# Products that nobody reads, put into TensorE's queue at three places of a fused attention and feed-forward kernel

## The chip, the cores and the metric

The kernel runs on one core of a Trainium2 chip. Its time is the device time of that core in microseconds (us). Three runs gave 560.56, 560.72 and 562.95 us, with a median of 560.72 us. The engines are called by the short names of the profile: PE is TensorE (PEld its weight loads), DVE is VectorE, ACT is ScalarE, POOL is GpSimd and SP is SyncE, which issues the DMAs.

## The reference

The reference computes attention with a memory term, and then a feed-forward layer on every token. B, H, S and D are 4, 8, 576 and 64; the layer has 2304 tokens, 512 columns and an inner width of 2048.

```python
scores = where(causal, -1e9, q @ k.T / sqrt(D));  a = softmax(scores)
local  = a @ v
q_p    = phi(q)                                   # phi(x) = where(x > 0, x, exp(x) - 1) + 1
mem    = (q_p @ M_prev) / (q_p @ z_prev + 1e-6)
x      = g * mem + (1 - g) * local                # g = sigmoid(beta), per head
out    = relu(x @ w_in) ** 2 @ w_out              # x as 2304 x 512
```

## The kernel before

**Work.** Attention runs in units: one unit is one batch, one pair of heads and some of the four 128-row query tiles. The feed-forward layer runs in blocks of 256 tokens. Block 0 holds the first 64 tokens of all four batches; its attention is computed ahead of everything by `first_tokens` in two groups of two batches (group 0 and group 1), so that block 0 can start while the units go on.

**Weights.** The weights come in 32 pieces of 128 x 512 floats of 64 bits, 512 KB each. `to_float` makes a 32-bit float tile `fc` of each piece: POOL or ACT (L200, L202) takes the low word, ACT (L205) the high word, and DVE (L207) joins them. Four pieces make a bundle: bundles 0, 2, 4, 6 are pieces of `w_in`, bundles 1, 3, 5, 7 of `w_out`. For each bundle `weight_scale` lets PE sum squares of the four pieces in a PSUM tile `gr` (L233), DVE takes a maximum of them (L236), PE spreads it over the partitions (L214) and DVE takes a maximum again (L215). From that come the scales `win_s` or `wout_s`, and `halves` makes the fp16 high part of each piece on ACT (L251) and its rest on DVE (L252): tiles w0 to w31. The name `kap` stands for the maxima of a `w_out` bundle, `win_e` for those of a `w_in` bundle.

**Group outputs.** `outputs(g)` transposes the exponentials (PE, `px`), copies them (ACT, `wx`, L391), multiplies with v (PE, `pv`, L395), and then DVE (L396, L397) and ACT make the fp16 rows `hl` that a DMA transposes into `xT`, the input of block 0.

**A unit.** PE writes scores (`sp`, L588), DVE masks them and takes maxima (L609), ACT takes exponentials (L631), PE transposes them (`pxa`, L648), ACT copies (`aF`, L653), PE multiplies with v (`acc`, L697), DVE adds to `feat` (L700). Unit 0 is the first of these; it has two query tiles.

**Order.** A list scheduler places every instruction on its engine's queue when the program is built, by estimated times; on the chip each engine works through its queue in order. Helpers such as `later` add an order without a wait: the instruction is placed behind the last one that `gate` names. PSUM tiles with one tag share buffers: `gr` and `up` (the first products of a block, L1000 to L1002) have two 2 KB buffers together, `px`, `pv`, `nm` and `oacc` two others. `fc` has 12 buffers, the raw pieces 7.

Of the kernel before, what the change touches and what calls it, by code (L numbers as in the profile page):

```python
# [8 lines left out]
F32 = mybir.dt.float32  # L9
F32R = mybir.dt.float32r  # L10
F16 = mybir.dt.float16
BF16 = mybir.dt.bfloat16
# [10 lines left out]
P = 128  # L23
# [58 lines left out]
WE = 8  # L82
WE2 = 16
WH = 11
AFTER = mybir.DependencyInfo(mybir.DependencyClass.NoSync, mybir.DependencyReason.DATA)
WHOLE = mybir.DependencyInfo(mybir.DependencyClass.Sync, mybir.DependencyReason.DATA)

# [13 lines left out]
def fused_kernel(ctx: ExitStack, tc: tile.TileContext, t0_d, kk_d, qv_d, beta, w_in, w_out, out):  # L101
    nc = tc.nc
    w_in = w_in.bitcast(U32)
    w_out = w_out.bitcast(U32)
    cp = ctx.enter_context(tc.tile_pool(name="cp", bufs=1))
# [6 lines left out]
    make_identity(nc, ident)  # L112
    identb = cp.tile([P, P], BF16, name="identb")
    nc.vector.tensor_copy(identb, ident)


    win_e = cp.tile([P, 4], F32, name="win_e")
# [50 lines left out]
    gate = {}  # L168

    def later(eng, x):  # L170
        if eng in gate:
            tc.add_manual_dep(x.ins, gate[eng].ins.name, AFTER, reason="first tokens lead")
        return x
# [19 lines left out]
    def to_float(n):  # L193
# [15 lines left out]
        )  # L209
        raw.pop(n)  # L210

    def over_partitions(x, al):

        nc.tensor.matmul(al, x.bitcast(BF16)[:, 1:2].to_broadcast([P, P]), identb, start=True, stop=True)  # L214
        nc.vector.reduce_max(out=x, in_=al, axis=AX.X)  # L215
# [9 lines left out]

    def weight_scale(g, w_is_out):

        gr = ps.tile([P, 2, P], F32, tag="up", name="gr", bufs=2)
        for k, n in enumerate(range(4 * g, 4 * g + 4)):
            x = fc[n].bitcast(BF16).rearrange("p (n t) -> p n t", t=2)[:, :, 1]  # L230
            for c in range(4):
                xc = x[:, c * P : (c + 1) * P]
                nc.tensor.matmul(gr[:, 0], xc, xc, start=k == c == 0, stop=k == c == 3)  # L233
        j = slice(g // 2, g // 2 + 1)
        x = kap[:, j] if w_is_out else win_e[:, j]
        nc.vector.reduce_max(out=x, in_=gr[:, 0], axis=AX.X)  # L236
        over_partitions(x, gr[:, 1])
        if w_is_out:
            root(x, 0x7E000000, 2, 2.0 ** (96 - 6))
            nc.vector.tensor_tensor(out=wout_s[:, j], in0=x, in1=x, op=ALU.mult)  # L240
            nc.vector.reciprocal(wout_s[:, j], wout_s[:, j])
            nc.vector.tensor_tensor(out=x, in0=x, in1=win_e[:, j], op=ALU.mult)
        else:
            root(x, 0x7F000000, 1, 2.0 ** (64 - 12))
            nc.vector.reciprocal(win_s[:, j], x)
# [67 lines left out]
    def first_tokens(tp, ahead):  # L313
# [23 lines left out]
        def pairs():  # L337
            return [(i, slice(h * D, (h + 1) * D)) for i in range(GN) for h in range(2)]
# [47 lines left out]
        def outputs(g):  # L386
            ex = tp.tile([P, GN, D], F32, tag="wx", name="wx", bufs=2)
            px = ps.tile([P, GN, D], F32, tag="acc", name="px0", bufs=2)
            for i, hd in pairs():
                nc.tensor.matmul(px[hd, i], et[g][hd, i], ident[hd, hd], start=True, stop=True)  # L390
            gate["s"] = nc.scalar.copy(ex, px)  # L391
            v, x, y = part(g, TV), ft[g], et[g]
            pv = ps.tile([P, GN, D], F32, tag="acc", name="pv0", bufs=2)
            for i, hd in pairs():
                gate["t"] = nc.tensor.matmul(pv[hd, i], ex[hd, i], v[hd, i], start=True, stop=True)  # L395
            nc.vector.tensor_tensor(out=y, in0=pv, in1=st[g][:, :, None].to_broadcast(bc), op=ALU.mult)  # L396
            nc.vector.tensor_tensor(out=x, in0=x, in1=y, op=ALU.add)  # L397
            xb = x.rearrange("p (b i) d -> p b (i d)", b=GB)
            hl = mo.tile([P, 2, GB, NP * D], F16, tag="hl", name="hl", bufs=2)
            ss, q, s = (tp.tile([P, GB], F32, tag=t, name=t, bufs=2) for t in ("s0", "qn", "sn"))  # L400
            for b in range(GB):
                nc.scalar.activation(hl[:, 0, b], xb[:, b], AF.Square, accum_out=ss[:, b : b + 1])
            nm = ps.tile([P, GB], F32, tag="acc", name="nm0", bufs=2)
            nc.tensor.matmul(
                nm, both.rearrange("p h x -> p (h x)"), ss.bitcast(BF16).rearrange("p (n t) -> p n t", t=2)[:, :, 1], start=True, stop=True
            )
            root(q, 0x7F000000, 1, 2.0**64 * XSC, nm)
            nc.vector.reciprocal(s, q)
            for b in range(GB):
                hi, lo, s1 = hl[:, 0, b], hl[:, 1, b], s[:, b : b + 1]  # L410
                gate["s2"] = nc.scalar.activation(hi, xb[:, b], AF.Copy, scale=s1)
                gate["v2"] = nc.vector.scalar_tensor_tensor(
                    out=lo, in0=xb[:, b], scalar=s1, in1=hi, op0=ALU.mult, op1=ALU.subtract
                )
            nc.sync.dma_start_transpose(out=xT[:, g], in_=hl.rearrange("p x b n -> p (x b n)"))
            for b in range(GB):
                hd = slice(b * D, (b + 1) * D)
                nc.scalar.activation(tok0[hd, g : g + 1], q[hd, b : b + 1], AF.Square, scale=WSC / HSC)
# [39 lines left out]
    def attention(b, p, tiles, ld, after, early, sfull, full, ap, ap_early):  # L458
# [163 lines left out]
        for i in [t for t in TORD if t in tiles]:  # L622
# [15 lines left out]
            if full:  # L638
# [3 lines left out]
                for b0 in range(0, 2 * nb, 4):  # L642
                    bn = min(4, 2 * nb - b0)
                    px = ps.tile([P, 4, P], F32, tag=PXT, name="pxa", bufs=2)
                    for x in range(bn):
                        h, c = divmod(b0 + x, nb)
                        c0, cw = cols[c]
                        nc.tensor.transpose(px[:cw, x, :n], e[:n, h, c0 : c0 + cw], ident)  # L648
                    lo = [x for x in range(bn) if (b0 + x) % nb == 0]
                    for x0, xn, pn in [(x, 1, D) for x in lo] + runs([x for x in range(bn) if x not in lo]):  # L650
                        dst, src = aT[:pn, b0 + x0 : b0 + x0 + xn, :n], px[:pn, x0 : x0 + xn, :n]
                        if PXE[b0 // 4] == "a":
                            nc.scalar.copy(dst, src)  # L653
                        else:
                            nc.vector.tensor_copy(dst, src)
# [293 lines left out]
    def moe(n):  # L949
# [43 lines left out]
        for j in range(NF // 2):  # L993
            need(1 + 8 * (j // 2 + 1))
            up = ps.tile([P, 2, BLK], F32, tag="up", name="up", bufs=2)
            for u in range(2):
                f = 2 * j + u
                uo = up[:, u].rearrange("p (g b q) -> p g b q", g=2, b=GB) if lead else up[:, u]
                for k in range(NK):
                    nc.tensor.matmul(uo, w_in_op(f, k, 0), x_op(k, 0), start=k == 0, stop=False)  # L1000
                    nc.tensor.matmul(uo, w_in_op(f, k, 0), x_op(k, 1), start=False, stop=False)  # L1001
                    nc.tensor.matmul(uo, w_in_op(f, k, 1), x_op(k, 0), start=False, stop=k == NK - 1)  # L1002
# [166 lines left out]
```

## Time and profile before

| | |
|---|---|
| median of 3 runs | 560.72 us |
| profiled execution | 560.21 us |
| its span, first to last instruction | 558.4 us |
| mean granted clock of TensorE | 0.976 of full |
| busy: PE, DVE, ACT, POOL | 523.7, 453.5, 410.0, 47.7 us |

The profiled execution takes 1.8 us more than its span, before the first and after the last instruction. Busy shares are averages over stages with different limits. PE is busy for 94% of the span, and without a gap from 70 to 100 us; before 70 us the weights are being made, and DVE and ACT are the engines that hardly pause. The granted clock has two levels, 1.00 (2.4 GHz) and 0.50 (1.2 GHz).

### The profile page before, as it was taken

The page shows a single profiled execution, that of the slowest core. Times are in us where ns is not written, and L with a number is a line of the kernel's source. Part 1 is how long each engine was busy: PE and PEld are TensorE (multiplying, and loading weights), DVE is VectorE, ACT ScalarE, POOL GpSimd, SP SyncE. Part 2 cuts the span into 40 slices and gives each one's busy share as a digit, 9 for nine tenths or more (in the row PEclk, how much of TensorE's full clock was granted, in tenths as well). Part 3 has the DMA queues.
Part 4 walks back from the last instruction along what each step waited for, and adds up shares of the span by engine and source line. Part 5 has one row for each costly group of instructions (what it writes and reads, how often), then busy time and mean ns, then how long its engine had stood idle before and what let it go on. Part 6 is the DMA issues. An engine that isn't in the chain of part 4 may idle for free.

```text
span 558.4 us, 12645 instructions
## 1 busy us (share of the span) xinstructions
PE 523.7 (94%) x4767; PEld 370.1 (66%) x4767; DVE 453.5 (81%) x1414; ACT 410.0 (73%) x883; POOL 47.7 (9%) x36
## 2 busy tenths in 40 slices
PE   4678999998999999999989999999999999999996
PEld 4555767756676776667756777667766766447776
DVE  6898978998999989999977878888686788745645
ACT  3699996875879889989877777888666734566252
POOL 2556420011010000000000000000000000000000
PEclk9965999999999999999999999999999999999999
DMA  8975922477778958979657376481745320100002
GB/s 305 406 274 191 329 80 69 103 143 172 129 144 174 208 136 144 193 151 204 119 103 154 113 138 123 76 141 50 114 92 81 89 44 2 39 1 1 1 1 75
DMA packets 133133, 71.38 MB, mean 128 GB/s; under 512 B 115408, under 2 KB 121552, under 8 KB 133072
## 3 DMA queue, kind: packets, MB, share of 16 engines
q1 hardware_dynamic: 133072, 70.57, 53.9%
q8 instruction: 37, 0.61, 0.4%
q14 instruction: 24, 0.20, 0.1%
HBM read 37.53 MB, written 4.72 MB: 76 GB/s over the span
## 4 chain that ended last, share of the span: by engine, by line
PE 37%; DVE 29%; ACT 20%; DMA 8%; issue 3%; POOL 1%; SPq 0%; ACTq 0%; DVEq 0%
DVE e L609 6%; ACT e L631 6%; PE seven L861 5%; DVE a L673 5%; PE oacc L972 4%; DMA aT<-a 4%; PE oacc L971 4%; PE oacc L973 4%; ACT a L671 3%; PE up L1000 3%; PE up L1002 3%; PE up L1001 3%; PE seven L833 2%; PE seven L834 2%; PE seven L832 2%
## 5 line engine op out<-in xcount | busy, mean ns | idle before, releaser
L1000 PE MATMUL up<-xT,w 128*128 128x256 f16 x448 | 123.4, 275 | 3.0 <-DMA xT<-hl 2.2
L1002 PE MATMUL up<-xT,w 128*128 128x256 f16 x448 | 123.4, 275 | 0.0
L1001 PE MATMUL up<-xT,w 128*128 128x256 f16 x448 | 123.3, 275 | 0.0
L631 ACT ACTIVATE e<-e,mx 128x320 f32<-128x320 f32 (+3 forms) x128 | 77.4, 605 | 49.3 <-DVE mx L609 22.9
L971 PE MATMUL oacc<-w,gh 128*128 128x512 f16 x224 | 85.0, 379 | 1.9 <-ACT gh L1009 1.9
L972 PE MATMUL oacc<-w,gh 128*128 128x512 f16 x224 | 84.9, 379 | 0.0
L973 PE MATMUL oacc<-w,gl 128*128 128x512 f16 x224 | 81.2, 379 | 0.5 <-DVE gl L1012 0.5
L673 DVE SCALAR_TENSOR_TENSOR a<-e,a 128x128 f16<-128x128 f32 x116 | 64.7, 568 | 11.6 <-ACT a L671 10.3
L671 ACT ACTIVATE a<-e 128x128 f16<-128x128 f32 x116 | 54.9, 522 | 1.6 <-DMA aT<-a 1.0
L1000 PEld LDWEIGHTS <-w 128*128 128x128 f16 x448 | 44.3, 99 | 14.3 <-DMA xT<-hl 2.6
L1001 PEld LDWEIGHTS <-w 128*128 128x128 f16 x448 | 44.3, 99 | 12.0 <-issue 1.7
L1002 PEld LDWEIGHTS <-w 128*128 128x128 f16 x448 | 44.2, 99 | 8.4 <-issue 0.4
L697 PE MATMUL acc<-vs,aT 128*128 128x64 f16 x1138 | 42.5, 193 | 6.6 <-DMA aT<-a 5.2
L609 DVE CUSTOM_DVE_ANT_0 e<-sp,mask 128x320 f32<-128x320 f32 (+3 forms) x128 | 47.2, 419 | 0.8 <-PE sp L588 0.4
L1006 ACT ACTIVATE r<-up,gam 128x512 f32<-128x512 f32 x48 | 32.4, 674 | 20.9 <-PE up L1002 18.3
L697 PEld LDWEIGHTS <-aT 128*128 128x128 f16 x1138 | 38.9, 98 | 12.5 <-DMA aT<-a 7.8
L1012 DVE TENSOR_TENSOR gl<-r,gh 128x512 f16<-128x512 f32 x56 | 39.0, 697 | 5.3 <-ACT gh L1009 4.7
L971 PEld LDWEIGHTS <-gh 128*128 128x128 f16 x224 | 21.9, 98 | 23.5 <-ACT gh L1009 2.7
L973 PEld LDWEIGHTS <-gl 128*128 128x128 f16 x224 | 21.7, 98 | 22.4 <-DVE gl L1012 1.5
L861 PEld LDWEIGHTS <-g 128*128 128x128 f16 x336 | 32.9, 98 | 4.2
L200 POOL TENSOR_SCALAR raw<-raw 128x512 uint32<-128x512 uint16 x16 | 33.0, 2063 | 27.9 <-DMA raw<-in_w_in_dram 11.8
L1007 ACT ACTIVATE r<-r 128x512 f32<-128x512 f32 x56 | 34.9, 623 | 0.7
(192 smaller groups left out, 1061.5 us busy)
## 6 DMA issues: line engine op xcount, KB each, us to landing
raw<-in_w_in_dram SPq DMA_DIRECT2D x16, 512.0 KB, 6.9
raw<-in_w_out_dram SPq DMA_DIRECT2D x16, 512.0 KB, 7.1
vv<-in_qv_dram SPq DMA_DIRECT2D x16, 320.0 KB, 3.1
kd<-in_kk_dram SPq DMA_DIRECT2D x16, 288.0 KB, 3.1
out_dram<-o SPq DMA_DIRECT2D x12, 256.0 KB, 2.0
qm<-in_qv_dram SPq DMA_DIRECT2D x8, 321.0 KB, 3.0
qm<-in_qv_dram SPq DMA_DIRECT2D x8, 193.0 KB, 4.1
vv<-in_qv_dram SPq DMA_DIRECT2D x8, 192.0 KB, 3.1
```

Of the source, the lines that this page charges most:

```text
L609: x = nc.vector.tensor_tensor_reduce(out=e[:, h, ka:kb], in0=sps[:, h, cs], in1=mask[:, 448 - q0 + ka : 448 - q0 + kb], scale=-0.125, scal ...
L631: ex = nc.scalar.activation(e[:n, h, :ke], e[:n, h, :ke], AF.Exp, bias=bs, scale=-1.0, accum_out=sm[:n, h : h + 1])
L671: nc.scalar.mul(av[:, :, o0 : o0 + w], x, SC)
L673: nc.vector.scalar_tensor_tensor(out=av[:, :, o0 + w : o0 + 2 * w], in0=x, scalar=SC, in1=av[:, :, o0 : o0 + w], op0=ALU.mult, op1=ALU.sub ...
L697: nc.tensor.matmul(acc[:n, h], lhs[:, :n], rhs, start=x == 0, stop=x == len(mms) - 1)
L861: mms.append(nc.tensor.matmul(x[blk] if len(blks) == 1 else x[:, blk], g[j][:, i0, a, blk, p], t_side(j, p, m, i1), start=j == js[0] and p ...
L971: nc.tensor.matmul(acc[t], gh[:, u, ts], w_out_op(f, 0), start=f == f0, stop=False)
L972: nc.tensor.matmul(acc[t], gh[:, u, ts], w_out_op(f, 1), start=False, stop=False)
L973: nc.tensor.matmul(acc[t], gl[:, u, ts], w_out_op(f, 0), start=False, stop=f == f1)
L1000: nc.tensor.matmul(uo, w_in_op(f, k, 0), x_op(k, 0), start=k == 0, stop=False)
L1001: nc.tensor.matmul(uo, w_in_op(f, k, 0), x_op(k, 1), start=False, stop=False)
L1002: nc.tensor.matmul(uo, w_in_op(f, k, 1), x_op(k, 0), start=False, stop=k == NK - 1)
```

## The change

At three places PE now multiplies a tile of zeros (`wide`, set once by POOL) with the identity and writes to PSUM columns that nobody reads, or that the next product overwrites:

- in `weight_scale`, 4 products of 256 columns behind each of pieces 4, 5 and 6, into the unused second half of `gr` (which grows from 1 KB to 2 KB of the same 2 KB buffer);
- in `outputs(1)`, 12 products of 512 columns into `pv` ahead of the real ones;
- in block 0, 8 products of 512 columns into the first `up` tile ahead of the real ones.

Where the name "x" is in `gate` when such a product is recorded, it is placed behind the last transpose recorded of unit 0. That holds for the first and the third place. Pieces 5, 6 and 7 of bundle 1 are summed behind such products in one PSUM tile, so their sums move too.

```diff
+SPARE = {4: 4, 5: 4, 6: 4}
...
+    wide = cp.tile([P, 4 * P], BF16, name="wide")
+    nc.gpsimd.memset(wide, 0.0)
...
+    def spare(out, n, new=True):
+
+        c = out.shape[-1] // P
+        for _ in range(n):
+            mm = nc.tensor.matmul(out, identb, wide[:, : c * P], start=new, stop=new)
+            if "x" in gate:
+                later("x", mm)
+
...
-        gr = ps.tile([P, 2, P], F32, tag="up", name="gr", bufs=2)
+        gr = ps.tile([P, 4, P], F32, tag="up", name="gr", bufs=2)
...
                 nc.tensor.matmul(gr[:, 0], xc, xc, start=k == c == 0, stop=k == c == 3)
+            spare(gr[:, 2:].rearrange("p a b -> p (a b)"), SPARE.get(n, 0), False)
...
             pv = ps.tile([P, GN, D], F32, tag="acc", name="pv0", bufs=2)
+            spare(pv.rearrange("p i d -> p (i d)"), (0, 12)[g])
...
-                        nc.tensor.transpose(px[:cw, x, :n], e[:n, h, c0 : c0 + cw], ident)
+                        x_ = nc.tensor.transpose(px[:cw, x, :n], e[:n, h, c0 : c0 + cw], ident)
+                        if me == 0:
+                            gate["x"] = x_
...
             up = ps.tile([P, 2, BLK], F32, tag="up", name="up", bufs=2)
+            if lead and j == 0:
+                spare(up.rearrange("p u b -> p (u b)"), 8)
```

The instructions move with it. In the rows below the line numbers of the changed kernel are larger (L233 becomes L244, L214 L225, L236 L248, L215 L226, L207 L210, L252 L264, L700 L715, L697 L712, L648 L661, L588 L601, L1000 L1017), and the numbers behind the names are those of single tiles.

PE around group 1 of the first tokens, before: `gr_529` is bundle 1 (pieces 4 to 7 are `fc_479` to `fc_527`; one product of the four of each piece is shown), `px0_306` and `pv0_324` belong to `outputs(1)`.

```order
L233 MATMUL gr_529<-fc_479 128x128
...
L233 MATMUL gr_529<-fc_494 128x128
...
L233 MATMUL gr_529<-fc_514 128x128
...
L233 MATMUL gr_529<-fc_527 128x128
...
L390 MATMUL px0_306<-ident_67,w_272 64x64 x16
...
L214 MATMUL gr_529<-identb_72,kap_77 128x128
L395 MATMUL pv0_324<-tr1_110,wx_305 64x64 x16
```

The same place now: `gr_543` is bundle 1, with piece 4 alone; the row of `pv0_326` from `wide_74` stands 12 times.

```order
L244 MATMUL gr_543<-fc_493 128x128
...
L417 MATMUL nm0_262<-s0_257,both_83 128x2
L402 MATMUL px0_308<-ident_67,w_274 64x64 x16
...
L219 MATMUL pv0_326<-wide_74,identb_72 128x512
...
L408 MATMUL pv0_326<-tr1_112,wx_307 64x64 x16
```

The sums of pieces 5 to 7 and the spreading of `kap` have left this place, and the 12 products stand between `px` and `pv`.

PE from the transposes of unit 0 to block 0, before: `pxa_499` holds the transposes of its second tile, `acc_481` the sums of its first, `gr_649` is bundle 3.

```order
L697 MATMUL acc_481<-vv_135,aF_419 128x64 x4
...
L214 MATMUL gr_649<-identb_72,kap_77 128x128
L697 MATMUL acc_481<-vv_135,aF_419 128x64 x2
...
L648 MATMUL pxa_499<-ident_67,e_412 64x128
L648 MATMUL pxa_499<-ident_67,e_412 128x128
...
L1000 MATMUL up_690<-xT_108,w0_463 128x256
```

The same place now; `fc_508` is piece 5 and stands for three times four rows (pieces 5, 6, 7), each behind four products into `gr_543` from `wide_74`; `gr_675` is bundle 3; the row of `up_716` from `wide_74` stands 8 times.

```order
L661 MATMUL pxa_513<-ident_67,e_426 128x128
...
L219 MATMUL gr_543<-wide_74,identb_72 128x256
...
L244 MATMUL gr_543<-fc_508 128x128
...
L225 MATMUL gr_675<-identb_72,kap_79 128x128
...
L225 MATMUL gr_543<-identb_72,kap_79 128x128
...
L219 MATMUL up_716<-wide_74,identb_72 128x512
...
L1017 MATMUL up_716<-xT_110,w0_477 128x256
```

Bundle 1 now ends between the transposes of unit 0 and block 0, behind 12 products from `wide`, and 8 more stand ahead of the first product of block 0. The maxima of bundles 1 and 3 are both spread there.

DVE behind unit 0, now: `feat_396<-acc_530` adds the second tile of unit 0, `w12_700` is of bundle 3 and `w4_580` of bundle 1. Before, the rests w4 to w7 stood some 60 rows further up, among the scores of unit 0 (L609).

```order
L264 SCALAR_TENSOR_TENSOR w11_648<-fc_614,win_s_77,w11_648 128x512
L248 TENSOR_REDUCE kap_79<-gr_543 128x1
L226 TENSOR_REDUCE kap_79<-gr_675 128x1
...
L715 SCALAR_TENSOR_TENSOR feat_396<-acc_530,sm_428,feat_396 128x64 x2
L264 SCALAR_TENSOR_TENSOR w12_700<-fc_655,wout_s_78,w12_700 128x512
...
L264 SCALAR_TENSOR_TENSOR w4_580<-fc_493,wout_s_78,w4_580 128x512
```

DVE at the maximum of bundle 4, the third `win_e`, before and now (`raw_1159` is piece 27, `raw_1101` piece 26):

```order
L207 SCALAR_TENSOR_TENSOR fc_1259<-raw_1159 128x512
L236 TENSOR_REDUCE win_e_74<-gr_945 128x1
L215 TENSOR_REDUCE win_e_74<-gr_945 128x1
```

```order
L210 SCALAR_TENSOR_TENSOR fc_1289<-raw_1101 128x512
L248 TENSOR_REDUCE win_e_76<-gr_979 128x1
L210 SCALAR_TENSOR_TENSOR fc_1293<-raw_1193 128x512
...
L226 TENSOR_REDUCE win_e_76<-gr_979 128x1
```

The maximum of bundle 4 now stands one piece earlier in DVE's queue: behind piece 26 and ahead of piece 27 (`fc_1293`).

## Rows read from the trace of the kernel before

**Rows 1.** Page, part 2: granted clock in 40 slices of 14 us, in tenths.

```profile
PEclk9965999999999999999999999999999999999999
```

**Rows 2.** Windows by stage: width, busy us (count) of each engine, granted clock, DMA.

```profile
26.90:37.10 10.20, 7.99 (x87) 6.58 (x87) 10.07 (x26) 9.64 (x19) 7.49 (x5) 0.50 0.74 240
40.50:57.60 17.10, 14.27 (x66) 10.36 (x67) 15.63 (x51) 16.70 (x46) 9.69 (x6) 0.50 0.63 211
70.00:100.00 30.00, 30.00 (x225) 21.18 (x225) 24.16 (x87) 24.21 (x65) 3.94 (x3) 1.00 0.22 67
26.90:68.50 41.60, 34.47 (x265) 26.83 (x264) 39.22 (x112) 40.59 (x92) 22.64 (x14) 0.67 0.78 267
```

**Rows 3.** Timeline of PE behind the third `win_e`: start, duration, engine, operation, wait.

```profile
69.96 0.27 PE L1000 MATMUL up<-xT,w 128*128 128x256 f16 x1 [0.38 <-DVE win_e L215]
```

**Rows 4.** Timeline of DVE, 35 to 70 us.

```profile
35.47 0.68 DVE L396 TENSOR_TENSOR w<-pv,t 128x512 f32<-128x512 f32 x1
...
38.47 0.74 DVE L252 SCALAR_TENSOR_TENSOR w<-fc,wout_s,w 128x512 f16<-128x512 f32 x1
...
40.51 2.07 DVE L252 SCALAR_TENSOR_TENSOR w<-fc,wout_s,w 128x512 f16<-128x512 f32 x3
...
60.08 0.47 DVE L700 SCALAR_TENSOR_TENSOR feat<-acc,sm,feat 128x64 f32<-128x64 f32 x2 [0.74 <-PE acc L697]
...
67.62 0.42 DVE L563 TENSOR_TENSOR feat<-pm,nm 128x256 f32<-128x256 f32 x1
67.96 1.13 DVE L207 SCALAR_TENSOR_TENSOR fc<-raw 128x512 uint32<-128x512 uint32 x1
69.01 0.28 DVE L236 TENSOR_REDUCE win_e<-gr 128x1 f32<-128x128 f32 x1
```

**Rows 5.** Timeline of ACT, 37 to 69 us.

```profile
37.27 2.54 ACT L251 ACTIVATE w<-fc,wout_s 128x512 f16<-128x512 f32 x4
...
47.31 2.56 ACT L251 ACTIVATE w<-fc,win_s 128x512 f16<-128x512 f32 x4
...
65.67 0.62 ACT L1007 ACTIVATE r<-r 128x512 f32<-128x512 f32 x1
...
67.95 0.67 ACT L205 ACTIVATE raw<-raw 128x512 f32<-128x512 f32 x1
```

**Rows 6.** Timeline of POOL, first microseconds.

```profile
0.86 0.58 POOL L129 MEMSET mask<- 128x576 bf16 x1
```

**Rows 7.** Timeline of PE in block 0: neighbouring products at either clock.

```profile
53.24 0.42 PE L1001 MATMUL up<-xT,w 128*128 128x256 f16 x1
53.46 0.42 PE L1002 MATMUL up<-xT,w 128*128 128x256 f16 x1
...
58.20 0.27 PE L1000 MATMUL up<-xT,w 128*128 128x256 f16 x1
58.31 0.27 PE L1001 MATMUL up<-xT,w 128*128 128x256 f16 x1
```

**Rows 8.** Timeline of PE, 26 to 53 us.

```profile
26.80 0.59 PE L233 MATMUL gr<-fc 128*128 128x128 bf16 x4 [2.11 <-DVE fc L207]
...
27.33 1.97 PE L390 MATMUL px<-ident,w 64*64 64x64 f32 x32
...
31.74 1.97 PE L395 MATMUL pv<-tr,wx 64*64 64x64 f32 x32 [2.21 <-ACT wx L391]
...
40.64 2.08 PE L588 MATMUL sp<-kd,qm 64*128 64x320 f32 x8 [1.63 <-DVE mx L609]
...
42.98 0.85 PE L648 MATMUL pxa<-ident,e 128*64 128x128 f32 x3
...
45.97 2.35 PE L697 MATMUL acc<-vv,aF 64*128 64x64 f32 x8
...
49.18 1.06 PE L648 MATMUL pxa<-ident,e 128*64 128x128 f32 x4
52.41 0.40 PE L1000 MATMUL up<-xT,w 128*128 128x256 f16 x1 [2.17 <-DMA xT<-hl]
```

**Rows 9.** Page, part 5: the masked scores on DVE, with the mean of one.

```profile
L609 DVE CUSTOM_DVE_ANT_0 e<-sp,mask 128x320 f32<-128x320 f32 (+3 forms) x128 | 47.2, 419 | 0.8 <-PE sp L588 0.4
```

## Prediction

> **What bounds the kernel now.** I read the slices of the page first. The reader is to see that the granted clock is lower only in the third and fourth slice, about 28 to 56 us [rows 1]; from there on it is full. So the change can pay, or cost, only ahead of some 70 us. Then I asked for busy times by stage. The clock is at 0.50 (1.2 GHz) from 26.9 to 37.1 us and from 40.5 to 57.6 us, 27.3 us in all; at 2.4 GHz the same work would have taken PE 13.65 us less, if nothing else bound it. But from 26.9 to 68.5 us ACT is busy for 40.59 of 41.60 us and DVE for 39.22: they make the weights, and they are the bound there, with pauses of 1.01 and 2.38 us. From 70 to 100 us PE is busy for 30.00 of 30.00 us: there it is the bound itself, and what starts it earlier or later shifts the rest by as much [rows 2]. Third I read the timelines for the hand-over between the two. PE starts that stage at 69.96 us behind DVE's maximum of bundle 4 [rows 3]. DVE takes it at 69.01, right behind the join of a piece whose high word ACT began at 67.95 and ended at about 68.5 [rows 4, 5]. So the time of the kernel hangs on when DVE and ACT get to that maximum, and on what PE makes them wait for on the way.
>
> **The change part by part.**
>
> *POOL's memset.* A fill of 128x576 costs 0.58 us [rows 6], so the new one of 128x512 some 0.5 us. It stands ahead of the mask, in the first two microseconds, where the kernel still waits for its inputs. Taken as 0; if all of it reached DVE's first masked scores, 0.5 us.
>
> *The 12 products in `outputs(1)`.* Neighbouring products of 256 columns start 0.22 us apart at the low clock and 0.11 at the high one [rows 7]. I take 512 columns as twice that, so the 12 last 5.2 or 2.6 us. In the trace PE ends `px` at 29.3 and waits 2.21 us for ACT's copy before `pv` at 31.74 [rows 8]. Piece 7's sums, for which PE had waited until 26.80, are gone from this place, so `px` can end at 28.8; then `pv` ends at 36.0 at the low clock throughout, and at 32.5 at the high one, instead of 33.7. Its reader L396 is reached by DVE at 35.47 [rows 4]. Bounds: 0.5 us late, or nothing gained, since weight joins stand ahead of L396 in either case. Taken as 0, the value in the middle of PE's ends.
>
> *Bundle 1 late.* Its four fp16 copies leave ACT's queue ahead of unit 0: 2.45 us, from 37.27 to 39.72 [rows 5]. Its four rests (0.67 each from start to start, 2.66 together) leave DVE's at 38.47 and 40.51 [rows 4]. Nothing is saved by this, they come back some 20 us later; but unit 0 starts earlier by ACT's 2.45: its first transposes at 40.5 instead of 42.98 [rows 8].
>
> *The stretch from there to block 0.* It now stands in one row on PE. At the low clock: transposes 0.65, scores of unit 1 2.0 (they stood ahead before), remaining transposes of the first tile 0.8, 16 sums of bundle 3 of 128 columns at 0.11 each 1.75, `acc` from 45.97 to 49.18 3.2, transposes of the second tile 1.0 [rows 7, 8]: 9.4 us, so 49.9. Then 12 products of 256 columns 2.6 and 12 of 128 columns 1.3: 53.8. At the high clock half of everything.
>
> *The new wait.* DVE's maximum `kap` of bundle 1 now stands behind the rest w11 and waits for these products. Behind it in DVE's queue stand the joins of pieces 16 to 19, the scales of bundles 1 and 3 (for which ACT's next eight copies wait) and the `feat` sum of unit 0's second tile. That sum waits for PE once more: for 8 products of 512 columns (3.5 or 1.75 us), 18 of block 0 (3.9 or 1.95) and `acc` (2.35 or 1.2).
>
> *Break-even.* In the trace DVE ends this `feat` sum at 60.5 [rows 4]. By then it had done one join (0.6), w4 to w7 (2.66) and w12 and w13 (1.34), which the new order still has to do: 4.6 us. So DVE is level if the sum ends at 55.9.
>
> *When it ends.* Low clock up to block 0, high from there: 53.8 + 0.4 (two maxima) + 3.5 + 1.95 + 1.2 + 0.4 (the sums) = 61.25, which is 5.35 late. High clock throughout: ACT's copies of bundle 2 end at 47.4 (49.87 less 2.45) [rows 5], DVE's last rest and the maximum follow at 48.2; 48.2 + 0.4 + 1.75 + 1.95 + 1.2 + 0.4 = 53.9, 2.0 early. Between them I take a rise in the middle of the stretch, at 45.2, because PE now has no wait in it: the two stretches of the trace in which it had none from a point on (from 31.74, and from 52.41) ended in a rise at 37.1 and 57.6, while 40.64 to 50.2, with waits in it, did not [rows 2, 8]. Then `acc` of the first tile, 3.7 us of low clock later, ends at 45.2 + 1.85 = 47.05. DVE needs 3.2 us more (two sums 0.4, three rests 2.0, two masked scores of 0.42 [rows 9]) and takes `kap` at 50.25, by when PE is done too (45.2 + 4.3 = 49.5). 50.25 + 0.4 + 1.75 + 1.95 + 1.2 + 0.4 = 55.95: level. Taken as 0, with -2.0 and +5.35 as ends.
>
> *The maximum of bundle 4 one piece earlier.* In the trace it came at 69.01, behind a join that stood from 67.96 on and waited for ACT, and behind a `feat` product at 67.62 [rows 4]. In the new order both stand behind it. What it needs of ACT, ACT had done by the point that it reached at 65.67 [rows 5]. PE still has 54 products of block 0 at 0.11 (5.9), and scores, memory products and bundle 4's sums (some 3.5) to do after the 55.5 at which `acc` ends, so it is there by 65 and doesn't bind. 69.01 - 67.62 = 1.4 gained, as long as DVE is level; 0 if another piece of DVE's work slips in.
>
> *Sum.* 0 + 0 + 0 - 1.4 on the profiled execution's 560.2 us (span 558.4 and 1.8 around it) is 558.8. The median of the runs lies 0.5 above the profiled execution, so 559.3 as a median.
>
> **Rivals.**
>
> *High clock all the way (faster).* If the 12 early products bring the clock up and it is up again from the start of the stretch, DVE is ahead by 2.0, within its pauses of 2.38 [rows 2]: with the 1.4 that is -3.4, 556.8 (557.3 as a median). For it: the rise at 37.1 came while PE ran without a wait from 31.74. Against it: PE waits for DVE's masked scores again, 1.63 us up to 40.64, and the clock fell at 40.5 in that wait [rows 2, 8].
>
> *Low clock up to block 0 (slower).* One mechanism: DVE stands at `kap` of bundle 1 while PE works off 12 products that nobody reads at half speed, and 8 more behind them. Price 5.35, less 1.4: +3.95, 564.2 (564.7 as a median). It makes the kernel slower from where the `feat` sum ends later than 57.3. For it: from 40.5 to 57.6 the trace has the low clock although PE was busy for 14.27 of 17.10 us [rows 2]. Against it: the waits in that stretch are gone from the new order.
>
> *It doesn't reach the end (no change).* ACT and DVE bind the stage with 40.59 and 39.22 of 41.60 us [rows 2]; PE's faster products only wait elsewhere, and the earlier maximum is eaten by ACT, which has more copies ahead of block 0's activations: 560.2 (560.7). Beside this stands a rule of the Trainium skill, page Perfetto Trace Analysis, section Optimization Strategies under Optimizing DMA Performance: when the matmul engine idles for other engines, work on those that block the critical path. By that rule filling PE's waits gives 560.2; the busy times agree with it up to the pauses that are left.
>
> **How the numbers follow.** Forecast 0.38, high clock 0.30, low clock 0.18, no change 0.14. About 0.5%, 2.8 us, is what a measurement can tell from no change here. Faster by more: 0.22 out of the high-clock case, 0.06 out of the forecast and 0.02 of the rest, 0.30. Slower by more: 0.15 out of the low-clock case and 0.03 of the others, 0.18. Within: 0.52. The range goes from 556.0 (the 1.4, all of DVE's 2.38, and 1 us from the order behind) to 564.0 (most of the low-clock case's price); the forecast's own is 557.5 to 561.5.
>
> **What would show it.** Right: a granted clock of 1.00 from about 45 us to the end; unit 0's first transposes near 40.5; DVE's `kap` of bundle 1 near 50; block 0's first real product at 52 to 53; the `feat` sum near 56; PE's first product behind the third `win_e` near 68.5, and no gap behind it. Wrong: DVE idle for over 2 us ahead of `kap`, the low clock at 50, ACT idle ahead of w12, or the earlier start at 68.5 lost again between 100 and 130 us, where the units come in.

## The result, and the profile after

The changed kernel takes 564.41 us in the median of 8 runs (563.21 to 566.27), the kernel before 560.27 us in 8 runs beside them (558.65 to 562.95). The ratio is 1.0073, with an interval of 1.0048 to 1.0097: 4.1 us slower. The forecast was 559.3 us with a range of 556.0 to 564.0; the time lies 0.4 us above that range, and on the other side of the kernel before. The profiled execution took 564.48 us, its span 562.7 us.

Up to 72 us the clock did what the forecast had hoped for. The page's slices and the windows of the changed kernel, as in [rows 1, 2]:

```profile
PEclk9689989999999999999999999999999999999999
```

```profile
20.00:31.10 11.10, 8.93 (x92) 6.11 (x91) 9.97 (x24) 8.31 (x19) 7.31 (x4) 0.50 0.98 387
31.10:41.40 10.30, 6.59 (x78) 4.55 (x76) 9.46 (x25) 10.30 (x26) 6.76 (x5) 1.00 0.85 258
41.40:44.80 3.40, 3.40 (x25) 2.43 (x24) 2.91 (x15) 2.69 (x11) 2.83 (x2) 0.50 1.04 403
44.80:72.00 27.20, 21.49 (x180) 17.29 (x181) 24.55 (x69) 26.02 (x55) 14.12 (x8) 1.00 0.83 255
72.00:75.50 3.50, 3.50 (x19) 2.51 (x18) 1.92 (x3) 3.50 (x8) 1.79 (x1) 0.51 0.01 2
154.00:157.40 3.40, 3.40 (x30) 2.73 (x27) 2.85 (x13) 2.23 (x5) 0.00 (x0) 0.50 0.48 74
```

From 44.8 us on the clock is full, but for 72.1 to 75.5 and 154.0 to 157.4. Before, it was at half from 40.5 to 57.6 and then full up to the end:

```profile
57.60:558.40 500.80, 485.35 (x4376) 339.66 (x4374) 404.41 (x1274) 367.26 (x791) 18.69 (x13) 1.00 0.51 109
```

The timeline of PE (start, duration, operation, wait before it), which answers [rows 3, 7, 8]:

```profile
40.13 0.52 PE L661 MATMUL pxa<-ident,e 128*64 128x128 f32 x3 [0.69 <-ACT e L644]
...
50.81 0.23 PE L225 MATMUL gr<-identb,kap 128*128 128x128 bf16 x1 [1.69 <-DVE kap L248]
51.01 1.89 PE L219 MATMUL up<-wide,identb 128*128 128x512 bf16 x8
52.73 0.27 PE L1017 MATMUL up<-xT,w 128*128 128x256 f16 x1
...
61.94 0.71 PE L565 MATMUL pm<-qm,pe 128*128 128x130 f32 x4 [0.93 <-DVE pe L518]
63.63 0.60 PE L661 MATMUL pxa<-ident,e 128*64 128x128 f32 x4 [0.98 <-ACT e L644]
...
69.39 0.23 PE L225 MATMUL gr<-identb,win_e 128*128 128x128 bf16 x1 [1.63 <-DVE win_e L248]
...
70.38 1.38 PE L712 MATMUL acc<-vv,aF 64*128 64x64 f32 x8 [0.48 <-DVE feat L576]
71.69 0.28 PE L1017 MATMUL up<-xT,w 128*128 128x256 f16 x1
```

DVE, answering [rows 4]:

```profile
50.48 0.28 DVE L248 TENSOR_REDUCE kap<-gr 128x1 f32<-128x128 f32 x1
...
56.37 0.48 DVE L715 SCALAR_TENSOR_TENSOR feat<-acc,sm,feat 128x64 f32<-128x64 f32 x2 [1.36 <-PE acc L712]
...
69.05 0.28 DVE L248 TENSOR_REDUCE win_e<-gr 128x1 f32<-128x128 f32 x1
69.25 0.68 DVE L210 SCALAR_TENSOR_TENSOR fc<-raw 128x512 uint32<-128x512 uint32 x1
...
69.93 0.40 DVE L576 TENSOR_TENSOR feat<-pm,nm 128x256 f32<-128x256 f32 x1
```

Up to 57 us this is the forecast to within 0.9 us. Then the first stretch of block 0's products, now at the full clock, is over at 59.9 us, PE stands for 0.93 and 0.98 us behind DVE and ACT, the third `win_e` comes no earlier (69.05 against 69.01), and PE works without a wait from 70.38 instead of 69.96, with half the clock from 72.1 to 75.5. PE was busy for all of these 3.4 us, so the clock took some 1.7 us of its work (an estimate from the row); with the 0.4 of its start that is about 2 of the 4.3 us between the two spans.

The rest lies where I had not looked. Waits of PE in two late stretches, of the changed kernel and then of the kernel before (what waited for what; us in total, times, longest):

```profile
PE acc L712 <- DMA aT<-a: 1.3, 1, 1.3
...
PE acc L712 <- DMA aT<-a: 1.7, 1, 1.7
```

The first stretch is 126 to 145 us, the second 414 to 430. In the first the kernel before has no wait of this kind, in the second one of 0.7 us:

```profile
PE acc L697 <- DMA aT<-a: 0.7, 1, 0.7
```

`a` is the matrix of weights that the DMA queue of SP transposes into `aT` for the later units; PE multiplies `aT` with v (`acc`). Over all of 76 to 556 us these waits are, in the changed kernel and then before:

```profile
PE acc L712 <- DMA aT<-a: 7.2, 5, 2.8
```

```profile
PE acc L697 <- DMA aT<-a: 5.2, 6, 1.7
```

The longest of the changed kernel, 2.77 us, ends at 153.3; the second fall of the clock follows it.

### The profile page after: what moved, and what is told of

It reads as the page before. It is cut to its first block, busy times and chain, and to the rows that moved or that the text cites. A ratio compares the mean times of both kernels' runs of the same rounds, so it can differ in the third digit from the quotient of the medians.

```text
span 562.7 us, 12735 instructions
## 1 busy us (share of the span) xinstructions
PE 524.8 (93%) x4799; PEld 371.2 (66%) x4799; DVE 451.9 (80%) x1414; ACT 410.0 (73%) x883; POOL 51.1 (9%) x37
## 4 chain that ended last, share of the span: by engine, by line
PE 39%; DVE 25%; ACT 13%; DMA 6%; issue 4%; SPq 0%; ACTq 0%; DVEq 0%
PE seven L876 5%; ACT e L644 5%; DVE a L688 5%; DVE e L622 5%; PE oacc L986 4%; PE oacc L988 4%; PE oacc L987 3%; DMA aT<-a 3%; PE up L1017 3%; PE up L1019 3%; PE acc L712 3%; PE up L1018 3%; ACT a L686 3%; PE seven L848 2%; PE seven L849 2%
## 5 line engine op out<-in xcount | busy, mean ns | idle before, releaser
L1017 PE MATMUL up<-xT,w 128*128 128x256 f16 x448 | 123.1, 275 | 0.0
L1017 PEld LDWEIGHTS <-w 128*128 128x128 f16 x448 | 44.2, 99 | 10.6 <-issue 0.4
L712 PE MATMUL acc<-vs,aT 128*128 128x64 f16 x1138 | 42.3, 193 | 7.8 <-DMA aT<-a 7.2
L712 PEld LDWEIGHTS <-aT 128*128 128x128 f16 x1138 | 39.0, 98 | 14.1 <-DMA aT<-a 8.9
L715 DVE SCALAR_TENSOR_TENSOR feat<-acc,sm,feat 128x64 f32<-128x64 f32 x128 | 29.3, 278 | 12.5 <-PE acc L712 12.3
L203 POOL TENSOR_SCALAR raw<-raw 128x512 uint32<-128x512 uint16 x16 | 35.5, 2217 | 28.0 <-DMA raw<-in_w_in_dram 14.6
```

The costliest lines, as they stand in the source:

```text
L712: nc.tensor.matmul(acc[:n, h], lhs[:, :n], rhs, start=x == 0, stop=x == len(mms) - 1)
```

## The experiments

Theory A put the loss on the scheduler's order, theory B on the products' own time and clock. Both could be tested cleanly. With the products at one column and without the order that `later` asks for, the scheduler builds the order of the kernel before, word for word in every queue (POOL's new fill apart); and once the order is fixed, each product can be made short or long. So order and length were varied one by one. When two kernels share an order, the start of each DVE instruction of one can be subtracted from the same one's of the other; that is the lag used below.

| run | order | products | instructions added on PE | median us | ratio, interval |
|---|---|---|---|---|---|
| changed kernel | new | 32 full | 62 | 564.41 | 1.0048 to 1.0097 |
| e1 | new | 32 short | 62 | 564.45 | 1.0050 to 1.0112 |
| e2 | old | 32 full | 63 | 564.32 | 1.0043 to 1.0099 |
| e3 | old | 12 full, 20 short | 63 | 565.23 | 1.0060 to 1.0125 |
| e4 | old | 8 full, 24 short | 63 | 565.10 | 1.0063 to 1.0124 |
| e5 | old | none, fill alone | 0 | 560.03 | 0.9968 to 1.0000 |
| e6 | old | 32 short | 63 | 563.78 | 1.0033 to 1.0078 |
| e7 | old | short | 256 | 561.78 | 0.9997 to 1.0029 |
| e8 | old | 32 full, rest short | 256 | 564.61 | 1.0039 to 1.0087 |
| e9 | old | none, 64 empty | 64 | 564.51 | 1.0056 to 1.0117 |
| e10 | new | 32 full, 64 empty | 126 | 566.00 | 1.0076 to 1.0117 |
| e11 | new | 32 full, 128 empty | 190 | 571.08 | 1.0164 to 1.0211 |
| e12 | new | 32 full, 192 empty | 254 | 568.05 | 1.0119 to 1.0161 |
| e13 | new | 32 full, rest short | 256 | 565.15 | 1.0058 to 1.0128 |
| e14 | new | short | 256 | 565.45 | 1.0063 to 1.0097 |
| e15 | old | 24 full, rest short | 256 | 562.07 | 1.0014 to 1.0058 |
| e16 | old | short | 128 | 570.74 | 1.0139 to 1.0211 |
| e17 | old | short | 192 | 565.76 | 1.0050 to 1.0103 |
| e18 | new | 32 full, rest short | 288 | 568.70 | 1.0108 to 1.0151 |

(The kernel before took 560.0 to 561.1 us beside them. The 32 products are 64 instructions; PE's program grows by 62 in the new order and by 63 in the old one, since two waiting instructions or one fall away.)

**Order against products: e1, e2.** e1, the new order with short products:

```diff
         fused_kernel(tc, *args)
+    size = {mm.ins.name: n for mm, n in zip(SP_, [1] * 32)}
...
+            _copy.replace(i, ins=(cut(i.ins[0], size[i.name]), i.ins[1]), outs=(cut(i.outs[0], size[i.name]),))
```

> All queues stand in the order of the changed kernel, word for word; only the 32 products are cut to one column each once that order is fixed, so TensorE works some 5.6 us less (12 x 0.21 + 12 x 0.11 + 8 x 0.21 at the high clock) and up to twice that at the low one. Theory A (the loss of 4.1 us is in the order that the scheduler built around the products: TensorE idle at 60 to 64 us, the third win_e behind two more pieces of DVE's work): the time stays at 563 to 566 us, over 0.5% above before. Theory B (the loss is the products' own time and what they do to the clock): back to 559 to 561 us. In between (561.5 to 562.5) both have a share. Low clock from 40 us to block 0 would show that the products held the clock up.

e2, the old order with full products:

```diff
-            mm = nc.tensor.matmul(out, identb, wide[:, : c * P], start=new, stop=new)
-            if "x" in gate:
-                later("x", mm)
+            mm = nc.tensor.matmul(out[:, :1], identb, wide[:, :1], start=new, stop=new)
+    size = {mm.ins.name: n for mm, n in zip(SP_, [512] * 12 + [256] * 12 + [512] * 8)}
```

> All queues stand in the order of the kernel before, word for word, with the 32 products added at the same three places at full width: 4 each behind the sums of pieces 4, 5 and 6 (which here stand early, ahead of group 1), 12 ahead of group 1's outputs, 8 ahead of block 0. Theory A: within 1 us of before, or up to 2 us faster if the clock stays up to block 0. Theory B: 563 to 566 us, since the products' 5.6 to 11 us of TensorE time are all there. What the theories share: the granted clock should rise earlier than at 57.6 us.

Measured: 564.45 and 564.32. e1 speaks against B, e2 against A. Whatever the two share with the changed kernel was neither.

**One place alone: e3, e4.** As e2, with other lengths:

```diff
+    size = {... zip(SP_, [512] * 12 + [1] * 20)}
```

> The order of the kernel before; only the 12 products ahead of group 1's outputs have their 512 columns, the other 20 have one column. They stand in a wait of 2.2 us and last 2.6 (high clock) to 5.2 us (low). Theory A: 559 to 561 us. Theory B: up to 3 us later than before, as far as they push group 1's outputs past 35.5 us, where DVE reads them.

```diff
+    size = {... zip(SP_, [1] * 24 + [512] * 8)}
```

> The order of the kernel before; only the 8 products ahead of block 0 have their 512 columns, the other 20 plus 4 have one column. Before block 0 TensorE waits 2.17 us for xT until 52.4; the 8 last 3.5 us at the low clock there, so block 0 starts up to 1.4 us later if they are issued only when the wait before them ends, and they may bring the rise of the clock forward from 57.6 to some 55. Theory A: 559.5 to 561 us. Theory B: 1 to 2 us slower.

Measured: 565.23 and 565.10, slower than either theory allows. With 8 full products the loss was no smaller than with 32. The common parts left were the fill, the new tile and the number of instructions.

**The fill, and the number of instructions: e5 to e9.** e5:

```diff
-SPARE = {4: 4, 5: 4, 6: 4}
+SPARE = {}
-            spare(pv.rearrange("p i d -> p (i d)"), (0, 12)[g])
+            spare(pv.rearrange("p i d -> p (i d)"), (0, 0)[g])
-                spare(up.rearrange("p u b -> p (u b)"), 8)
+                spare(up.rearrange("p u b -> p (u b)"), 0)
```

> No product at all: only the tile wide with POOL's fill (0.53 us, which moves the identity matrix from 1.47 to 1.94 us) and the four-part gr tile; every queue but POOL's has the order of the kernel before, and TensorE's program has the same length. The four runs so far were 4 to 5 us slower than before in either order and with long or short products, so neither the order nor the products' time is the cause that they share. Theory D (the fill or the moved tiles are that cause): 564 to 565 us. Theory C (the cause is the 63 more instructions in TensorE's program, which move the fetches of its code, 16 KB and about 1 us each, against the transposes of aT): 559.5 to 561.5 us, as before.

e6 is e2 without the lengthening:

> The order of the kernel before in all queues, the tile wide and its fill, and the 32 products with one column each: TensorE's program is 63 instructions (4032 bytes) longer, its busy time under 1 us longer. Theory C: 563.5 to 565.5 us. Theory D: the same as the run with the fill alone. Theory B (products' own time): 560 to 561 us.

e7 puts 193 copies of the short products behind them, e8 does so with the 32 at full length:

```diff
+            for c in range(more.get(k, 0)):
+                out.append(sized(i, 1, name=..., sync_info=None))
```

> As the run with 32 one-column products, with 193 copies of them more: TensorE's program is 256 instructions, 16384 bytes, longer than before, the length of one fetch, so each later fetch stands where it stood before against the work. The copies cost TensorE some 0.03 us each, 5 us in all, in places where it waits (between early sums, ahead of group 1's outputs, ahead of block 0). Theory C: back to 559.5 to 562 us. Theory D: 564 us or more. If any added instruction costs, whatever its place: 565 us or more.

> As the run with 256 more instructions, but with the 32 products at their full 512 and 256 columns (5.6 us of TensorE at the high clock), in the order of the kernel before. Theory C: the fetches stand as in the kernel before, and what is left is the products' own effect: with the earlier rise of the clock that the run in the old order showed (0.991 as the mean) 557 to 560.5 us, which would beat both kernels. Theory D: 564 us or more.

e9 is the kernel before with one edit:

```diff
+    for _ in range(64):
+        nc.tensor.nop(hint="n", nofuse=True)
     with _tile.TileContext(nc, schedule_with_timeline_sim=True) as tc:
```

> The kernel before, unchanged in every queue, with 64 empty instructions (no operands, no products, no fill) at the head of TensorE's program, where TensorE waits for its first input anyway: 4096 bytes more. Theory C (the place of the code fetches against the transposes of aT): 563 to 565 us, with waits of acc for aT near 132, 160 and 420 us, each 2 to 3.5 us behind a fetch. If it is the added products in any form (the 32 one-column ones too) and not their place in the code: 560 to 561 us.

Measured: the fill costs nothing (560.03); 32 short products cost 3.2 us (563.78), and 64 empty instructions alone, with nothing else changed, 4.5 us (564.51); 256 instructions cost 1.2 us or nothing (561.78, the interval reaches below 1). Cost doesn't grow with the number, it goes by the place. The lag of DVE behind the kernel before, in us, at times of that kernel:

```
                 100   128   140   360   385   415   435   550
e5    (0)       -0.9  -0.9  -0.6  -0.6  -0.8  -0.8  -0.9  -0.9
e7    (256)     +1.0  +0.8  +0.9  +0.8  +0.8  +0.8  +0.7  +0.7
e8    (256)     +4.1  +3.7  +3.8  +3.7  +3.8  +3.7  +3.7  +3.7
e6    (63)      +0.5  +0.1  +0.7  +0.7  +1.4  +1.4  +4.3  +4.3
e9    (64)      -2.6  -2.9  -1.9  -1.5  -0.7  -0.7  +1.8  +1.8
e16   (128)     +2.2  +1.8  +2.5  +4.3  +6.0  +6.6  +9.0  +9.0
e17   (192)     -0.6  -0.9  -0.2  +3.3  +3.4  +3.3  +4.8  +4.8
```

From 100 us to the end the lag moves by 0.4 us at most with 0 or 256 instructions added, and by 3.8 to 6.8 us with 63, 64, 128 or 192. (The runs that are not in the table fit less sharply: 0.7 us in e15 with 256, and 2.4, 4.6 and 3.0 us in e2 to e4 with 63. Each row is one execution; that of e9 took 562.02 us, 2.5 less than its median.) The reader can see why in the DMA view of 412 to 418 us, in slices of 0.15 us: first the kernel before (GB/s, queue), then e9 (busy tenths, GB/s, queues).

```profile
GB/s 196 215 218 218 203 205 224 213 215 220 215 218 217 218 218 215 171 128 159 212 224 213 220 196 203 220 220 217 213 217 203 189 227 93 0 0 0 0 14 176
...
q1 hardware_dynamic: 4250, 1.07, 97.4%
```

```profile
DMA  9999999999999999999999900100008999999999
GB/s 203 215 218 218 217 217 218 218 218 217 218 157 147 159 253 239 213 210 317 207 215 159 39 0 0 9 7 10 10 10 184 292 292 285 282 241 247 213 212 213
...
q1 hardware_dynamic: 4219, 1.06, 124.2%
q8 instruction: 1, 0.02, 1.0%
```

Queue 1 carries the transposes at some 217 GB/s. In e9 one packet of queue 8 falls into them, a fetch of 16 KB of instructions that starts at 414.8 us, and from 415.4 to 416.5 us the core's DMA engines move 0 to 10 GB/s: the transposes stand still. In the kernel before no fetch falls into this stretch (they start at 405.0 and 419.6; the zeros at its end stand where it has no transposes). In the changed kernel one starts at 419.1, and its `acc` gets `aT` late at 422.5. Its DMA view of 418 to 423 us, in slices of 0.125 us:

```profile
GB/s 135 139 189 228 221 209 209 205 348 190 205 201 92 20 0 0 0 2 6 10 8 10 10 8 18 268 285 293 293 291 261 279 270 248 211 229 217 219 195 193
...
q8 instruction: 1, 0.02, 1.5%
```

It is so throughout: in the 20 traces 55 fetches start while queue 1 carries next to nothing but transposes, and behind 54 of them queue 1 falls below 15 GB/s for 0.6 us. The kernel before has such stops too, the fetch at 419.6 makes one; what differs is which of them PE has to wait out. Plain copies aren't stopped. In the kernel before a fetch starts at 26.3 us among the loads of the weights (26 to 30 us):

```profile
GB/s 492 369 410 533 328 410 328 369 451 369 328 410 328 451 410 328 451 328 451 410 410 369 451 369 492 410 369 410 369 410 451 451 410 369 410 451 369 410 451 328
```

Of the three waits that e9 was to show, two came (129.3 us, 2.4 behind a fetch, and 417.9, 3.1 behind one), the one near 160 didn't. And the wait is not the whole price. Of the 2.5 us that e9 loses from 415 to 435 us, the longer wait makes 1.0 (1.61 us against 0.66). The other 1.6 is the clock, at half right behind that wait while PE is busy throughout:

```profile
418.10:421.50 3.40, 3.40 (x55) 3.08 (x52) 2.12 (x14) 1.41 (x4) 0.00 (x0) 0.50 0.51 98
```

e3, e6 and e16 have the same fall between 420 and 426 us and lose 2.5 to 2.9 us there; e2, e4 and e17 have none there and lose 1.0 to 1.5. With 0 or 256 instructions added, the old order has no such fall behind 80 us but for the last 2.

The page counts 37 such fetches in either kernel:

```profile
q8 instruction: 37, 0.61, 0.5%
```

37 times 16 KB are 0.61 MB, and PE's program before has 9,599 instructions, 259 for each fetch: one fetch is 256 instructions of 64 bytes, so 256 added instructions move every later fetch by a whole one, and 63 by a quarter. The Trainium skill, page Runtime: NRT & Kernel Launch, section Instruction fetch mechanics, states blocks of 256 instructions, with which this agrees. It also calls the cost of crossing from one block to the next mostly hidden. For the engine that fetches this agrees too: from 424 to 552 us, with 7 fetches, the kernel before shows no wait of PE. For the transposes beside it the runs contradict.

e8 failed its expectation for another reason: its whole loss is there by 60 us. In this order the 8 products stand ahead of `acc` and of DVE's `kap`; with 37 copies behind them, and at the low clock, they held PE from 45.82 to 50.3, and DVE waited 5.4 us for `kap` instead of 0.9.

**The changed order at other places of the fetches: e10 to e14, e18.** e10 to e12 are the changed kernel with the edit of e9 (64, 128, 192):

> The changed kernel, unchanged in every queue, with 64 empty instructions at TensorE's head: its code starts half a fetch later than in the kernel before (62 + 64 instructions). In the changed kernel acc waits for aT for 1.25 us at 134.6 and for 1.72 us at 422.5, each behind a fetch by 2.2 and 3.4 us. Theory C: these two waits go, others may come; 561 to 564 us. If the order is what costs the 4.1 us: 564 to 565 us in all three phases.

> As the run before it, with 128 empty instructions: three quarters of a fetch. Theory C: another time than with 64 or none, 561 to 565 us. Order alone: 564 to 565 us.

> As the runs before it, with 192 empty instructions: with the 62 of the change that is 254, so the fetches stand, but for two instructions, where they stand in the kernel before. Theory C: the waits at 134.6 and 422.5 us (3.0 us together) go, 561 to 562 us. What stays above 560.5 then is the price of the order and of the products. Order alone: 564 to 565 us.

Measured: 566.0, 571.1, 568.1. Theory C (the place of the fetches) said that the times differ, and with the changed kernel's 564.4 they do by 7 us; but e12 was to be 561 to 562. Its two waits behind fetches are gone but for 0.3 us, and from 60 us to the end it gains 2.9 us on the changed kernel; but 192 empty instructions take 9.3 us at the head, of which 6.3 are still there at 60 us. So I put copies of short products where PE has time instead, 76, 60 and 58 of them (the edit of e7 on the changed kernel), with full and with short products:

> The changed kernel with its full products and its own order in every queue; 194 one-column copies of the products are added where TensorE has time (76 ahead of group 1's outputs, 60 between the sums of bundle 1, 58 ahead of block 0; 0.03 us each), so that TensorE's program is 256 instructions longer than in the kernel before and the later fetches stand where they stand there. The run with 192 empty instructions at the head lost 6.4 us before 74 us by them, and from there to 443 us gained 3.1 us on the changed kernel. Theory C: those 3 us without the price: 561 to 563 us, of which 1 to 2 us by the copies. If the order and the products cost the 4.1 us whatever the fetches: 564 to 566 us.

> As the run before it, but with the 32 products at one column: the order of the changed kernel alone. The difference to that run is the products' own time and clock: 0 if the two runs agree within 1 us; 2 to 4 us less here if the products cost what they last. Against before (560.0 to 560.7): what stays is the price of the order, 1 to 2 us by the waits that remain in the changed kernel's trace (2.02 us at 118.2 and 2.77 us at 153.3, against 1.26 us at 148.0).

Measured: 565.15 and 565.45. The two agree, so the products' length costs nothing here either. But C fell for the changed order: with the fetches where they stand in the kernel before it is no faster. PE's waits in e13, 126 to 145 us, no longer have the one for `aT`:

```profile
PE oacc L988 <- ACT gh L1028: 0.9, 1, 0.9
PE sp L603 <- DVE mx L624: 0.7, 1, 0.7
PE oacc L990 <- DVE gl L1031: 0.6, 1, 0.6
```

and there is none from 414 to 430; and the lag of DVE behind the changed kernel falls by 0.5 us from 128 to 140 us and by 1.0 from 415 to 440. But between the two it rises by 1.4, and it ends at +0.2. An eighth of a fetch further on (90, 70 and 66 copies):

> The changed kernel with its full products and its own order, and 226 one-column copies: 288 instructions more than before, a whole fetch and an eighth, between the two places at which it has taken 565.2 (256) and 564.4 us (62). If the changed order has a place of the fetches at which it is as fast as the kernel before, it is likeliest between its two best: 560 to 562.5 us. If it has none, 564 to 566 us.

Measured: 568.70, over the 564 to 566 of either case. I found no place at which the new order is as fast as the old one at its best.

**What the products bring, and two more places: e15 to e17.** e15 is e7 with `[512] * 12 + [256] * 12 + [1] * 8` and with no copies ahead of block 0; e16 and e17 are e7 with 65 and 129 copies.

> The order of the kernel before with 24 of the products at full width (12 of 512 columns ahead of group 1's outputs, 12 of 256 between the sums of pieces 4 to 6), the 8 ahead of block 0 at one column, and 193 copies: 256 instructions more. In that order the 8 stand ahead of DVE's wait for kap, where they cost 4.3 us in the run with 256 more instructions. Theory C: 560 to 562 us; 558 to 559.5, better than both kernels, if the earlier rise of the clock reaches the end.

> The order of the kernel before, the 32 one-column products and 65 copies of them: TensorE's program is 128 instructions longer, half a fetch. With the kernel before (0), the run with 32 short products (63), this one (128) and the run with 256 it gives the time by the place of the fetches alone. Theory C: a time of its own, anything from 560 to 568 us, with every lasting jump against the trace of before standing behind a fetch. If each added instruction costs the same: 562 us, since 63 cost 3.2 and 256 cost 1.2 us.

> The order of the kernel before, the 32 one-column products and 129 copies of them: TensorE's program is 192 instructions longer, three quarters of a fetch. It completes four places of the fetches in this order (0: 560.6 or, with copies, 561.8; 63: 563.8; 128: 570.7), to be set beside the four of the changed kernel's order (254 or 256: 565.2 to 568; 62: 564.4; 126: 566.0; 190: 571.1). If the order itself costs 4 us: 561 to 564 us here, and the mean over the places is 4 us lower than that of the changed order. If the order costs nothing in the mean: 565 to 571 us.

Measured: 562.07, beside 561.78 with short products: the mean granted clock rose from 0.975 to 0.980, and the time didn't move. e16 took 570.74, e17 565.76. Not every lasting jump of e16 stands behind a fetch, as theory C had it: it loses 2.4 us from 74 to 100 us, where PE shows no wait; there the clock had been at half from 70.6 to 74.0. In e16 PE waits for `aT` four times from 280 to 430 us, in the kernel before three times (second fence):

```profile
PE acc L712 <- DMA aT<-a: 7.3, 4, 2.4
```

```profile
PE acc L697 <- DMA aT<-a: 2.9, 3, 1.7
```

At four places of the fetches (256, 63, 128, 192) the old order takes 561.8, 563.8, 570.7 and 565.8 us, in the mean 565.5. The new order takes 565.2, 564.4, 566.0 and 571.1 (256, 62, 126, 190; the last two with empty instructions at the head, of whose cost 0.2 and 0.3 us are left at 100 us), in the mean 566.7. That is 1.2 us apart, where an order that costs 4 us at every place would make 4. The kernel before stands at the best of the four places that were tried in its order. No version with products beat it.

## Why the prediction was wrong

- *What bounds the kernel.* PE is full after 70 us, ACT and DVE bind ahead of it: right. (The 13.65 us is too much: PE was busy for 22.26 of the 27.3 us, which makes 11.1. No term uses it.) "So the change can pay, or cost, only ahead of some 70 us" was the failure. It was argued from the clock, as if products were the only thing that 32 products add. They also add 62 instructions to PE's program and move others, and these act on everything behind them. Its signs of being wrong named a loss from 100 to 130 us, but "0 + 0 + 0 - 1.4" has no term for one. In the profiled executions 564.5 us stand against the forecast's 558.8: 1.4 that was not gained, 0.4 of PE's start, some 1.7 of the clock at 72.1 (an estimate), and 2.2 behind that. In the old order, instructions that do next to nothing cost 3.2 to 4.5 (e6, e9).
- *The memset at 0*: right (e5). *The 12 products at 0*: right; `pv` ended at 33.4 instead of 33.7, the clock having risen at 31.1.
- *Bundle 1 late.* First transposes at 40.13 (40.5 was said); *the rise of the clock* at 44.8 (45.2), though the half clock ahead of it began only at 41.4; *`kap`* at 50.48 (50.25); block 0 at 52.73 (52 to 53): right.
- *Break-even.* The `feat` sum ended at 56.85 instead of 55.95, 0.9 late.
- *The maximum one piece earlier, -1.4*: mis-sized, 0 by the row of 69.05. The join (69.25) and the `feat` product (69.93) do stand behind it, as said. But the `feat` sum of unit 0 was 0.9 late, and from its end to the maximum DVE took 12.2 us without a pause, where the forecast has 11.7. PE then waited for that `feat` product: it went on at 70.38, and with block 0 at 71.69, where 68.5 was said.
- *The rivals.* "High clock all the way" came true for the clock up to 72 us and not for the time. In the new order, two pairs of runs that differ in the products' length alone (changed kernel and e1, e13 and e14) differ by 0.0 and 0.3 us. In the old order longer products never made it faster: 0.5 us slower (e2 against e6), 0.3 (e15 against e7, whose copies also stand elsewhere), 1.3 to 1.5 (e4 and e3 against e6) and 2.8 (e8 against e7). So for a gain by the products "it doesn't reach the end" was right. This agrees with the rule of the Trainium skill that the prediction names (page Perfetto Trace Analysis, section Optimization Strategies). "Low clock up to block 0" didn't come.

What stays open is what costs the changed kernel its 4.1 us: the place of the fetches alone and the order alone each make 3 to 4.5, and the two don't add. With the fetches of the kernel before, the new order costs 3.4 us (565.15 against 561.78, both with copies); with those of the change it costs nothing (564.4 against 563.8 and 564.5). The first is shown as a difference of times alone. The waits that are longer in e13 than in e7 (2.76 against 1.31 us for `aT` at 153.2, 1.57 against 0.39 for `mx` at 118.4) would make 2.6 of it if they lasted, but no run took them away. All eight traces of the new order have a fall of the clock to half between 117 and 159 us. The one at 154.0 in the changed kernel had no lasting price: e1, without it, is 1.2 us ahead of it in DVE's lag at 150 us and 1.3 at 170. The one at 72.1 had, as far as these two executions show: e1, without it, goes from 0.6 us behind at 74 to 1.4 ahead at 100.

## What to carry to other kernels

Filling an engine's waits to keep its clock up pays only where that engine ends last; read that first. And in a tuned kernel with a long program, count the instructions that an edit adds: they move the fetches of all later code against the DMA transposes, and here the time moved by up to 10 us with them in the old order and by up to 7 in the new. Test such an edit beside the same number of empty instructions, and again with a whole fetch of short ones where the engine waits, before its time is put down to what it does. A transpose that comes late can cost more than PE's wait for it, where the clock falls behind that wait (1.0 and 1.6 us in e9).

## What I had not expected of the hardware

A fetch of 16 KB of instructions takes 0.9 to 1.4 us in the kernel before. From some 0.6 us after its start the transposes of the core's DMA queue come down to 0 to 10 GB/s, from 217, for about 1.1 us (e9, 415.4 to 416.5 us); loads of weights kept on at 328 to 533 GB/s beside one. 64 empty instructions in a program of some 9,600 made it 0.87% slower (interval 0.56 to 1.17), 256 with operands 0.13% (-0.03 to 0.29). At the head of PE's queue, 64, 128 and 192 empty instructions (e10 to e12) made DVE 0.6, 4.7 and 9.3 us late at 12 us: some 70 ns for each beyond the first 64.
